# A Fourier filter of eight sequences and a top-k expert layer: transform stages packed differently, gate logits taken from the spectrum, outputs built only for the kept tokens

## The chip, the cores and the metric

One core of one Trainium2 chip runs the whole program: TensorE (PE, with PEld for its weight loads), VectorE (DVE), ScalarE (ACT), GpSimd (POOL), SyncE (SP) and 16 DMA engines. The metric is the device time of one execution in microseconds (us), median of several runs. All data are float32 in DRAM, and products that matter are float32 on TensorE.

## The reference

Eight sequences of 2496 tokens with 256 channels pass through a global filter (a real Fourier transform along the tokens, a product with a filter per frequency and channel, the transform back). The result, 19968 tokens, goes to a layer of 8 experts. Each token's expert is the largest of 8 logits; each expert keeps at most 80 tokens, those of the largest gate value; every other output row is zero.

```python
X = np.fft.rfft(x, axis=1); Y = X * (filt_r + 1j * filt_i)
y = np.fft.irfft(Y, n=2496, axis=1).reshape(19968, 256)
logits = y @ w_gate; expert_idx = argmax(logits); gate_w = softmax(logits)[expert_idx]
for e in range(8):                      # capacity 80
    tok_idx = the 80 tokens of expert e with the largest gate_w
    out[tok_idx] = gate_w[tok_idx] * (relu(y[tok_idx] @ w1[e]) @ w2[e])
```

So at most 640 of the 19968 rows of y are used for more than their logits. In the reference's inputs all eight experts are full (640 kept tokens), and by sequence there are 84, 64, 74, 90, 80, 74, 85 and 89 of them.

## The kernel before

The kernel has three parts: the filter for all sequences (lines 120 to 290), the choice of tokens (`select`, line 369 on), and the experts (lines 309 to 366). Tables for the transforms are made on the host as constants in DRAM and loaded at the start on ACT's DMA queue (`load_tables`, line 150).

A sequence of 2496 = 39 x 64 tokens is transformed in two stages, and back in two. Stage 1 (`stage1`, line 178) takes the transform of length 39: a chunk of x with 78 rows (39 positions by 2 halves h) and 4 columns of 256 channels is the moving side of two matmuls with 512 columns against the constant `wf_t` (78 x 80). The result goes from PSUM (tile `pa`) by DVE or ACT into `t1` and on POOL's DMA queue to a scratch tensor `d1` in DRAM. There are 8 chunks for a sequence. Stage 2 (`load_t2`, line 196, and `stage2`, line 207) reads `d1` back with the 64 positions on the partitions, 128 rows of real and imaginary parts, and works in 10 steps u of two residues s: `pb` is the transform of length 64 (constant `d_t`, 256 moving columns), DVE multiplies it with two copies of the filter (line 222), and `pc` (four matmuls of 256 columns a step, constant `e_t`) is the complex product's sum and the inverse transform of length 64 in one. The result goes to scratch `d2`. Stage 3 (`stage3`, line 246) reads `d2` in 8 chunks of 80 rows: `pd` (512 columns) is the inverse transform of length 39, whose rows go by POOL's queue to `y_rows` in DRAM; `pt` computes the same transposed, with the channels on the partitions, and `pl` takes the 8 logits of each token from that, in 64 matmuls of 8 columns for a sequence. The logits stay in `lg`.

The loop of lines 277 to 290 runs ten rounds: in round i, chunk by chunk, stage 1 of sequence i and stage 3 of sequence i - 2; then stage 2 of sequence i - 1, and then four DMAs that write zeros over that sequence's part of the output (`zero_out`, line 167, POOL's queue, put behind the last write of `d2`). SP's queue loads x, `d1` and `d2`.

After the rounds SP loads weights of five experts, and `select` runs: gates by softmax, keys transposed to (token, expert) rows, a search for the 80th largest key of each expert in 9 steps of 7 counts on DVE (line 482), prefix sums, and a compaction by one-hot products (lines 575 to 593) that leaves for every expert slot the token's number and gate. Then, expert by expert, POOL gathers the 80 rows of `y_rows` by their numbers, two layers run on TensorE, and POOL scatters the rows to the output.

A float32 matmul stands in the trace as two MATMUL instructions, called passes below, each with its LDWEIGHTS.

Of the kernel before, what the change touches and what calls it, by code (L numbers as in the profile page):

```python
# [10 lines left out]
AL = mybir.AluOpType  # L11
# [17 lines left out]
JC = 4  # L29
NCH = NJ // JC  # L30
SG = 4
E, FF = 8, 1024
NDB, NFC = C // 128, FF // 128


def dft_tables():
# [6 lines left out]
    wf = np.zeros((N1, 2, 2, NS, 2))  # L43
    wi = np.zeros((2, NS, 2, N1, 2))
    for h in range(2):
        wf[:, h, :, :, h] = w
        wi[:, :, h, :, h] = v.transpose(0, 2, 1) / S

    # The upper half of q holds the conjugates of frequencies above S / 2.
# [9 lines left out]
    d = d.reshape(128, NS, 128)  # L59
    back = d.transpose(2, 1, 0)  # L60
    e = np.zeros((128, 2, NS, 128))
    e[:, 0] = back
    e[0:64, 1] = back[64:128]
    e[64:128, 1] = -back[0:64]
    f32 = np.float32
    return (wf.reshape(NR, NK).astype(f32), wi.reshape(NK, NR).astype(f32),
            d.astype(f32), e.astype(f32))
# [3 lines left out]
def kernel(  # L71
# [14 lines left out]
    wf_host, wi_host, d_host, e_host = dft_tables()  # L86
# [4 lines left out]
    y_dram = nc.dram_tensor("y_rows", (N, C), F32, kind="Internal").ap()  # L91

    def behind(ins, other):
        tc.add_manual_dep(ins.ins, other.ins.name, mybir.DependencyInfo(
            mybir.DependencyClass.NoSync, mybir.DependencyReason.DATA), reason="order of work")

    consts = ctx.enter_context(tc.tile_pool(name="consts", bufs=1))

# [17 lines left out]
    # Logits of token 2496 b + 32 r + j at [r, 32 b + j, :].  # L116
    T = B * NJ
    lg = consts.tile([NR, T, E], F32, name="lg")

    with ExitStack() as fctx:  # L120
# [5 lines left out]
        xpool = pool("xp", 6)  # L126
        t1pool = pool("t1", 3)
        t2pool = pool("t2", 6)
        xfpool = pool("xf", 2)
        ppool = pool("pp", 4)  # L130
        gpool = pool("gp", 2)
        t4pool = pool("t4", 4)
        ypool = pool("yp", 3)
        ytpool = pool("yt", 2)
        dpool = pool("dram", 2, DRAM)
        fps = pool("fps", 5, PSUM)
        tps = pool("tps", 2, PSUM)
        lps = pool("lps", 1, PSUM)

        wf_t = tpool.tile([NR, NK], F32, name="wf_t")  # L140
        nc.scalar.dma_start(out=wf_t, in_=wf_dram.ap())
        d_t = tpool.tile([128, NS, 128], F32, name="d_t")
        e_t = tpool.tile([128, 2, NS, 128], F32, name="e_t")
        wi_t = tpool.tile([NK, NR], F32, name="wi_t")
        wg = tpool.tile([128, NDB, E], F32, name="wg")
        f_t = [tpool.tile([128, NS, C], F32, name=f"filt{i}") for i in range(2)]
        ZR = S // 4
        zero_t = tpool.tile([128, ZR * C // 128], F32, name="zero_t")

        def load_tables():  # L150
            nc.scalar.dma_start(out=d_t, in_=d_dram.ap())
            for k, filt in enumerate((filt_r, filt_i)):
                for half in range(2):
                    for q in range(2):
                        off, step = (0, C) if q == 0 else (N1 * C, -C)
                        p0 = 64 * half + 32 * q
                        nc.scalar.dma_start(
                            out=f_t[k][p0:p0 + 32],
                            in_=bass.AP(tensor=filt.tensor, offset=filt.offset + off,
                                        ap=[[N1 * C, 32], [step, NS], [1, C]]))  # L160
            nc.scalar.dma_start(out=e_t, in_=e_dram.ap())
            nc.scalar.dma_start(out=wi_t, in_=wi_dram.ap())
            nc.scalar.dma_start(
                out=wg, in_=moe_w_gate.rearrange("(k p) e -> p k e", p=128))
            nc.gpsimd.memset(zero_t[:], 0.0)

        def zero_out(b):
            for i in range(4):
                r0 = b * S + i * ZR
                ins = nc.gpsimd.dma_start(  # L170
                    out=out[r0:r0 + ZR, :].rearrange("r d -> (r d)").rearrange(
                        "(p m) -> p m", p=128),
                    in_=zero_t[:])
                behind(ins, st["last"])

        st = {}

        def stage1(b, ch):
            if ch == 0:
                st["d1", b] = dpool.tile([2 * NS, N2, C], F32, name=f"d1_{b}", tag="d1")  # L180
            d1_rows = st["d1", b].rearrange("a (h n) c -> (a h) n c", h=2)
            xt = xpool.tile([NR, JC, C], F32, name=f"x_{b}_{ch}", tag="x")
            nc.sync.dma_start(
                out=xt,
                in_=bass.AP(tensor=x.tensor, offset=x.offset + (b * S + ch * JC) * C,
                            ap=[[NJ * C, NR], [C, JC], [1, C]]))
# [20 lines left out]
        def stage2(b, u):  # L207
            if u == 0:
                st["d2", b] = dpool.tile([2 * NS, N2, C], F32, name=f"d2_{b}", tag="d2")
# [429 lines left out]
```

## Time and profile before

| | |
|---|---|
| median of 3 runs (lowest, highest) | 1460.03 us (1459.12, 1461.13) |
| span of the profiled execution | 1459.7 us |
| time outside that span, by the median | 0.3 us |
| PE busy / PEld / DVE / ACT / POOL | 1107.9 / 758.3 / 440.0 / 197.6 / 199.0 us |
| bytes moved by DMA | 173.27 MB |
| mean granted clock of TensorE | 0.627 of full speed |

The profile comes from one execution. Busy time is the sum over an engine's instructions; the granted clock is 0.5 for 1.2 GHz and 1.0 for 2.4 GHz, and shows 1.00 before the first change of it is recorded, whatever the clock is. A window's line gives the stretch, its length, the busy us (and instructions) of PE, PEld, DVE, ACT and POOL in it, the granted clock, the DMA share and the GB/s, so a stage can be read by itself. The DMA share is the mean over 16 DMA engines.

### The profile page before, as it was taken

How to read it: one execution, taken by the hardware profiler on the slowest of the kernel's cores; microseconds unless marked ns; L12 is line 12 of the kernel's file. 1: busy time of each engine (PE TensorE's matmuls, PEld its weight loads, DVE VectorE, ACT ScalarE, POOL GpSimd, SP SyncE). 2: the span in 40 equal slices, each digit the busy share in tenths (PEclk: the TensorE clock that was granted, in tenths of full speed). 3: DMA queues.
4: the chain of work that ended last, by engine and by line, in shares of the span. 5: the costliest groups of instructions: out<-in, count | busy, mean ns of one | idle time of the engine just before them, and what ended most of it. 6: DMA issues, size and time to landing. Idle time of an engine off the chain costs nothing. (4 is left out here: it accounts for less than half of the span.)

```text
span 1459.7 us, 10929 instructions
## 1 busy us (share of the span) xinstructions
PE 1107.9 (76%) x4234; PEld 758.3 (52%) x4234; DVE 440.0 (30%) x644; ACT 197.6 (14%) x342; POOL 199.0 (14%) x288
## 2 busy tenths in 40 slices
PE   6395999599969996997899699969969800002497
PEld 1153667466836674666566466747757600001386
DVE  1131113111311140113111311221121189999700
ACT  0121112111301130113011211221121100000001
POOL 1011001100110020002000200010020040001711
PEclk9997557655755585559555855675575555555579
DMA  9986324632563255336433732362162170000050
GB/s 230 236 255 210 107 89 122 199 107 80 142 189 107 80 146 182 98 92 179 150 98 91 222 98 63 88 198 72 35 178 72 59 264 0 0 0 0 7 173 30
DMA packets 71902, 173.27 MB, mean 119 GB/s; under 512 B 8235, under 2 KB 39723, under 8 KB 71467
## 3 DMA queue, kind: packets, MB, share of 16 engines
q0 software_dynamic: 24064, 84.17, 19.5%
q1 hardware_dynamic: 44224, 79.18, 18.5%
q10 hardware_dynamic: 3563, 9.23, 2.8%
q8 instruction: 33, 0.54, 0.2%
q14 instruction: 18, 0.15, 0.0%
HBM read 89.06 MB, written 83.49 MB: 118 GB/s over the span
## 5 line engine op out<-in xcount | busy, mean ns | idle before, releaser
L257 PEld LDWEIGHTS pt<-wi_t,t 80*128 80x128 f32 x1024 | 231.2, 333 | 171.2 <-DMA t<-d 124.5
L257 PE MATMUL pt<-wi_t,t 80*128 80x78 f32 x1024 | 229.8, 419 | 118.5 <-DMA t<-d 118.5
L190 PE MATMUL pa<-x,wf_t 78*80 78x512 f32 x256 | 222.5, 1029 | 35.4 <-ACT t L193 15.6
L263 PE MATMUL pd<-t,wi_t 80*78 80x512 f32 x256 | 231.7, 1061 | 0.0
L268 PEld LDWEIGHTS pl<-wg,yt 128*78 128x78 f32 x1024 | 152.2, 257 | 76.5 <-issue 76.5
L193 DVE COPY t<-pa 80x512 f32<-80x512 f32 x96 | 65.6, 686 | 393.2 <-PE pa L190 349.2
L259 DVE COPY yt<-pt 128x312 f32<-128x312 f32 x128 | 61.8, 482 | 387.2 <-PE pt L257 387.2
L265 ACT COPY y<-pd 78x512 f32<-78x512 f32 x128 | 74.4, 581 | 620.0 <-PE pd L263 620.0
L233 PE MATMUL pc<-p,e_t 128*128 128x256 f32 x640 | 156.0, 386 | 0.6 <-DVE p L222 0.5
L268 PE MATMUL pl<-wg,yt 128*78 128x8 f32 x1024 | 141.9, 274 | 0.0
L222 DVE TENSOR_TENSOR p<-xf,filt 128x512 f32<-128x512 f32 x160 | 103.4, 688 | 109.5 <-ACT xf L218 109.5
L233 PEld LDWEIGHTS pc<-p,e_t 128*128 128x128 f32 x640 | 121.8, 193 | 23.3 <-DVE p L222 6.6
L190 PEld LDWEIGHTS pa<-x,wf_t 78*80 78x80 f32 x256 | 57.0, 246 | 129.1 <-issue 81.4
L270 POOL DMA_DIRECT2D y_rows<-y x64 | 34.0, 531 | 533.1 <-ACT y L265 533.1
L214 PE MATMUL pb<-t,d_t 128*128 128x256 f32 x320 | 97.8, 436 | 0.0
L263 PEld LDWEIGHTS pd<-t,wi_t 80*78 80x78 f32 x256 | 57.4, 255 | 76.4 <-issue 76.4
L482 DVE TENSOR_SCALAR_CACHE_REDUCE junk<-keyT,thr 128x1248 bf16<-128x1248 f32 x63 | 95.3, 1512 | 5.2 <-ACT keyT L451 3.0
L487 PE MATMUL pc<-cnt,grp 128*128 128x7 f32 x18 | 5.3, 365 | 105.1 <-DVE junk L482 105.1
L242 POOL DMA_DIRECT2D d<-g x80 | 50.0, 629 | 197.8 <-ACT g L238 189.4
L214 PEld LDWEIGHTS pb<-t,d_t 128*128 128x128 f32 x320 | 70.4, 223 | 12.5 <-issue 1.1
L194 POOL DMA_DIRECT2D d<-t x64 | 33.4, 523 | 294.6 <-ACT t L193 159.7
L238 ACT COPY g<-pc 128x512 f32<-128x512 f32 x80 | 46.8, 585 | 99.0 <-PE pc L233 97.2
(112 smaller groups left out, 469.2 us busy)
## 6 DMA issues: line engine op xcount, KB each, us to landing
d<-t POOLq DMA_DIRECT2D x64, 320.0 KB, 3.7
t<-d SPq DMA_DIRECT2D x80, 256.0 KB
d<-g POOLq DMA_DIRECT2D x80, 256.0 KB, 3.8
t<-d SPq DMA_DIRECT2D x64, 320.0 KB
x<-in_x_dram SPq DMA_DIRECT2D x64, 312.0 KB
out_dram<-zero_t POOLq DMA_DIRECT2D x32, 624.0 KB, 8.0
y_rows<-y POOLq DMA_DIRECT2D x64, 312.0 KB, 3.3
w<-in_moe_w_dram SPq DMA_DIRECT2D x16, 1024.0 KB
```

Source lines behind the costliest of these rows:

```text
L190: nc.tensor.matmul(out=ps[0:NK], lhsT=wf_t, rhs=xt[:, 2 * i:2 * i + 2, :], start=True, stop=True)
L193: copy(out=t1[:, 2 * i:2 * i + 2, :], in_=ps[0:NK])
L214: nc.tensor.matmul(out=ps[:, i, :], lhsT=d_t[:, s, :], rhs=st["t2", b, s // SG][:, s % SG, :], start=True, stop=True)
L222: nc.vector.tensor_tensor(out=pt, in0=xf, in1=f_t[k][:, 2 * u:2 * u + 2, :], op=AL.mult)
L233: nc.tensor.matmul(out=ps[:, i, :], lhsT=e_t[:, k, s, :], rhs=pr[k][:, i, :], start=(k == 0), stop=(k == 1))
L242: st["last"] = nc.gpsimd.dma_start(out=st["d2", b][a0:a0 + SG].rearrange("s n c -> n s c"), in_=st["g"][64 * p:64 * p + 64])
L257: nc.tensor.matmul(out=pt[:, j, :], lhsT=t4[:, j, 128 * cb:128 * cb + 128], rhs=wi_t, start=True, stop=True)
L259: nc.vector.tensor_copy(out=yt[:, cb], in_=pt)
L263: nc.tensor.matmul(out=ps[0:NR], lhsT=wi_t, rhs=t4[:, 2 * i:2 * i + 2, :], start=True, stop=True)
L265: nc.scalar.copy(out=yr[:, 2 * i:2 * i + 2, :], in_=ps[0:NR])
L268: nc.tensor.matmul(out=pl[0:NR, JC * ch + j, :], lhsT=yt[:, cb, j, :], rhs=wg[:, cb, :], start=(cb == 0), stop=(cb == NDB - 1))
L482: nc.vector.tensor_scalar(out=junk[:], in0=keys, scalar1=thr[:, j:j + 1], scalar2=None, op0=AL.is_ge, op1=AL.add, accum_out=cnt[:, j:j + 1],)
```

## The change

Stage 1 takes 117 rows (39 positions by 3 parts h of 22 columns) against a constant with 120 columns, in six chunks (five of 4 columns, one of 2), so 11 matmuls of 512 columns for a sequence instead of 16. A chunk of x is loaded by three DMAs of 39 rows. Its results are all copied by ACT and written on ACT's DMA queue.

Stage 2 swaps the sides: a 128-channel block of `t2` is the weight side and `d_t` (128 columns) the moving side, so the spectrum comes out with the channels on the partitions. The filter, turned once into this form by 80 transposes, is multiplied on DVE straight from PSUM, and POOL does the two sums of the complex product. A new step `turn`, two steps u later, multiplies with `gi`, which is the identity (128 columns) beside the 8 gate columns: one matmul of 136 columns turns the spectrum back and also takes its product with `w_gate`. ACT copies both, POOL adds the two halves of the gate product into `z` and writes the spectrum to `yf` in DRAM. Stage 3, `y_rows` and the scratch `d2` are gone. Instead `logits`, for two sequences at a time and 16 columns, takes the inverse transform of the gate product alone, in five parts laid between the steps of a later sequence.

The order of all this is written out by hand: in step u of sequence b, stage 2 of b, stage 1 of sequence b + 1 (u below 6), `turn` of step u - 2, from u = 7 the loads of `t2` of b + 1, and a part of `logits`.

The zeros are written after this loop, 32 DMAs on SP's queue; three experts' weights are loaded behind them and the next two after the new stage below. `select` works on 128 partitions (two blocks of 39 used) and has more at its end: which of 128 places of its sequence a kept token takes, and lists of the tokens by sequence.

New between `select` and the experts: `back`, once for each sequence. It gathers the 128 rows (2560 floats each) of a table of the inverse transform that belong to the sequence's kept tokens, loads the sequence's spectrum `yf` (2.6 MB), transposes the gathered rows (20 transposes, copied by DVE and ACT in turn), and 20 matmuls of 256 columns give y for those 128 places, written to `y_sel`. Where a sequence has over 128 kept tokens, a branch taken at run time (`tc.If`) does up to four more lists, each with all eight sequences. The experts gather from `y_sel`.

```diff
-NR = 2 * N1
-NK = 4 * NS
+H3, J3 = 3, 22
+NP1, NM1 = N1 * H3, 2 * NS * H3
+CHUNKS = [(0, 4), (4, 4), (8, 4), (12, 4), (16, 4), (20, 2)]
...
         def stage1(b, ch):
...
+            for i in range(jn // 2):
                 ps = fps.tile([128, 2, C], F32, name=f"pa_{b}_{ch}_{i}", tag="f")
+                nc.tensor.matmul(out=ps[0:NM1], lhsT=wf_t, rhs=xt[:, 2 * i:2 * i + 2, :],
                                  start=True, stop=True)
-                copy = nc.scalar.copy if i == 1 and ch % 2 else nc.vector.tensor_copy
-                copy(out=t1[:, 2 * i:2 * i + 2, :], in_=ps[0:NK])
-            nc.gpsimd.dma_start(out=d1_rows[:, JC * ch:JC * ch + JC, :], in_=t1)
+                nc.scalar.copy(out=t1[:, 2 * i:2 * i + 2, :], in_=ps[0:NM1])
+            nc.scalar.dma_start(out=st["d1", b][:, j0:j0 + jn, :], in_=t1[:, 0:jn, :])
...
         def stage2(b, u):
...
+            for i in range(2):
+                s = 2 * u + i
+                for cb in range(NDB):
+                    nc.tensor.matmul(
+                        out=ps[:, i, cb], rhs=d_t[:, s, :], start=True, stop=True,
+                        lhsT=st["t2", b, s // SG][:, s % SG, 128 * cb:128 * cb + 128])
+            for k in range(2):
...
+                nc.vector.tensor_tensor(
+                    out=pt, in0=ps[:].rearrange("p s c r q -> p (s c) r q"),
+                    in1=f.unsqueeze(2).to_broadcast([128, 2 * NDB, 2, NQ]), op=AL.mult)
...
+            nc.gpsimd.tensor_tensor(out=yt[:, :, 0, :], in0=pr[0][:, :, 0, :],
+                                    in1=pr[1][:, :, 1, :], op=AL.subtract)
+            nc.gpsimd.tensor_tensor(out=yt[:, :, 1, :], in0=pr[0][:, :, 1, :],
+                                    in1=pr[1][:, :, 0, :], op=AL.add)
...
+        def turn(b, u):
...
+                    nc.tensor.matmul(
+                        out=ps[:, i, 136 * cb:136 * cb + 136], rhs=gi[:, cb, :],
+                        lhsT=yt[:, 2 * i + cb].rearrange("p r q -> p (r q)"),
+                        start=True, stop=True)
...
+            nc.scalar.copy(out=ys[:, m:m + 2, :], in_=ps[:, :, 0:ZW])
...
+                nc.gpsimd.dma_start(out=yf[b][:, SG * g:SG * g + SG, :], in_=ys[:, :, E:E + C])
...
+            for b in range(B):
+                for u in range(NU + LATE):
+                    if u < NU:
+                        stage2(b, u)
+                    if b + 1 < B and u < len(CHUNKS):
+                        if xs:
+                            load_x(*xs.pop(0))
+                        stage1(b + 1, u)
+                    if u >= LATE:
+                        turn(b, u - LATE)
+                    if b + 1 < B and u >= len(CHUNKS) + 1 and u - len(CHUNKS) - 1 < NS // SG:
+                        load_t2(b + 1, u - len(CHUNKS) - 1)
+                    if b % 2 == 0 and b > 0 and u in (1, 2, 4, 5, 7):
+                        logits(b // 2 - 1, (1, 2, 4, 5, 7).index(u))
+            for part in range(5):
+                logits(B // 2 - 1, part)
...
+    def back(mp, mps, nm, loads, put, idx, start=True, stop=True, acc=None, pad=False):
...
+        nc.gpsimd.indirect_dma_start(
+            out=gt[:], out_offset=None, in_=rows[:, :],
+            in_offset=bass.IndirectOffsetOnAxis(ap=idx, axis=0), **kw)
+        yb = loads()
...
+        for g in range(NS // SG):
...
+                nc.tensor.transpose(ps[:, i, :], gt[:, 128 * s:128 * s + 128], ident[:])
+            copy = nc.vector.tensor_copy if g % 2 == 0 else nc.scalar.copy
+            copy(out=wt[:, SG * g:SG * g + SG, :], in_=ps[:])
...
+        for s in range(NS):
+            nc.tensor.matmul(po[:], lhsT=wt[:, s, :], rhs=yb[:, s, :],
+                             start=(start and s == 0), stop=(stop and s == NS - 1))
...
+        n_more = nc.values_load(more[0:1, 0:1], min_val=0, max_val=E * cap)
+        with tc.If(n_more > 0):
...
+                for t in range(NX):
+                    ix = spill_lists(tc, mp, mps, t, cap, nof, ohb, iota, idxg)
+                    for b in range(B):
+                        po = back(mp, mps, f"x{t}_{b}",
...
-            out=xg[:], out_offset=None, in_=y_dram[:, :],
+            out=xg[:], out_offset=None, in_=y_sel[:, :],
```

## Rows read from the trace of the kernel before

**Rows 1.** Windows by stage; engines' busy us (instructions), then clock, DMA share, GB/s.
```profile
0.00:91.80 91.80, 56.37 (x65) 15.57 (x66) 16.72 (x28) 5.16 (x8) 10.31 (x25) 1.00 0.94 240
280.00:374.60 94.60, 94.60 (x313) 59.38 (x314) 14.58 (x26) 11.62 (x20) 7.90 (x15) 0.50 0.33 96
374.60:405.70 31.10, 30.98 (x129) 25.17 (x128) 14.13 (x23) 11.60 (x20) 5.94 (x11) 0.91 0.54 147
405.70:420.00 14.30, 0.16 (x1) 0.16 (x1) 0.60 (x1) 0.00 (x0) 2.98 (x6) 0.56 0.99 323
1163.60:1381.20 217.60, 32.49 (x314) 27.16 (x314) 199.24 (x233) 3.58 (x5) 47.17 (x22) 0.50 0.14 50
1381.20:1459.70 78.50, 66.32 (x400) 56.60 (x400) 6.53 (x16) 7.25 (x16) 14.88 (x16) 0.83 0.31 98
```

**Rows 2.** Timeline of PE: start us, us, line, shapes, passes, idle before and its releaser.
```profile
66.11 25.89 PE L190 MATMUL pa<-x,wf_t 78*80 78x512 f32 x30 [3.72 <-DVE t L193]
...
234.43 3.76 PE L214 MATMUL pb<-t,d_t 128*128 128x256 f32 x8
...
244.27 1.89 PE L233 MATMUL pc<-p,e_t 128*128 128x256 f32 x8
246.00 1.03 PE L214 MATMUL pb<-t,d_t 128*128 128x256 f32 x4
...
280.00 3.70 PE L257 MATMUL pt<-wi_t,t 80*128 80x78 f32 x16 [14.70 <-DMA t<-d]
...
1386.41 13.86 PE L332 MATMUL ph<-xs,w 128*128 128x80 f32 x64
...
1413.64 3.69 PE L332 MATMUL ph<-xs,w 128*128 128x80 f32 x32
```

**Rows 3.** Groups by line and shape: busy us, mean ns of one, idle before and releasers.
```profile
L222 DVE TENSOR_TENSOR p<-xf,filt 128x512 f32<-128x512 f32 x160 | 103.4, 688 | 109.5 <-ACT xf L218 109.5
L265 ACT COPY y<-pd 78x512 f32<-78x512 f32 x128 | 74.4, 581 | 620.0 <-PE pd L263 620.0
L242 POOL DMA_DIRECT2D d<-g x80 | 50.0, 629 | 197.8 <-ACT g L238 189.4 <-issue 8.5
L465 POOL TENSOR_TENSOR res<-gw,vv 78x256 f32<-78x256 f32 x1 | 0.8, 809 | 0.1
L449 PE MATMUL pk<-ident,key 78*128 78x78 f32 x16 | 2.3, 339 | 24.8 <-issue 24.8
L424 DVE TENSOR_TENSOR sh<-lg,mx 78x2048 f32<-78x2048 f32 x1 | 2.3, 2286 | 0.0
L599 DVE SCALAR_TENSOR_TENSOR tok<-slot,tok 80x8 f32<-80x8 f32 x1 | 0.2, 164 | 0.0
```

**Rows 4.** Windows of 1 us after which the clock is high, in stage 2 and among the experts.
```profile
240.00:241.00 1.00, 1.00 (x5) 0.85 (x5) 0.14 (x1) 0.00 (x0) 0.00 (x0) 0.93 0.92 278
1404.00:1405.00 1.00, 1.00 (x6) 0.74 (x5) 0.00 (x0) 0.00 (x0) 0.00 (x0) 0.95 0.54 217
```

**Rows 5.** DMA queues of the page: packets, MB, share of 16 engines' span.
```profile
q0 software_dynamic: 24064, 84.17, 19.5%
q1 hardware_dynamic: 44224, 79.18, 18.5%
```

**Rows 6.** Two windows without any compute, DMA alone (columns as in Rows 1).
```profile
268.00:272.00 4.00, 0.00 (x0) 0.00 (x0) 0.00 (x0) 0.00 (x0) 0.40 (x1) 0.50 1.01 386
274.00:278.00 4.00, 0.00 (x0) 0.00 (x0) 0.00 (x0) 0.00 (x0) 0.00 (x0) 0.50 1.03 287
```

**Rows 7.** Timeline of ACT at the start: its queue issues the tables.
```profile
1.77 25.48 ACTq L157 DMA_DIRECT2D filt<-in_filt_r_dram  x4
```

**Rows 8.** The experts' gathers of 80 rows of 1 KB, issue to landing.
```profile
DMA to landing us min/median/max: 2.5/4.0/5.9
```

**Rows 9.** Timeline of POOL: the last scatter, the last instruction before the end.
```profile
1452.73 0.91 POOL L350 DMA_INDIRECT out_dram<-ys,idxs  x1 [2.54 <-ACT ys L349]
```

**Rows 10.** POOL's elementwise product of the compaction, all calls: shortest, median, longest ns.
```profile
L580 POOL TENSOR_TENSOR vals<-vv,oh_bf x8: 2758/5335/5337, 1193.1 to 1369.7; 78x1536 bf16<-78x1536 bf16 x8
```

More of the change, by code (lines that the diff above doesn't have):

```diff
@@ L42, in dft_tables @@
     v[0, :, 0], v[1, :, 0] = 1.0, 0.0
[L43 to L47, printed above, removed]
+    v /= S
+    wf = np.zeros((H3, N1, 2, NS, H3))
+    for h in range(H3):
+        wf[h, :, :, :, h] = w
     kap = np.where(q[:, None] < 32, s + N1 * q[:, None], s + N1 * (95 - q[:, None]))
@@ L150, in load_tables @@
[L150 to L153, printed above, removed]
+        t2pool = pool("t2", 8)
+        ppool = pool("pp", 2)
+        ytpool = pool("yt", 3)
+        yspool = pool("ysp", 3)
+        zpool = pool("zp", 2)
+        d1pool = pool("d1p", 3, DRAM)
+        fps = pool("fps", 4, PSUM)
+        yps = pool("yps", 2, PSUM)
+        wf_t = tpool.tile([NP1, NM1], F32, name="wf_t")
@@ new lines, with load_tables @@
+        d_t = tpool.tile([128, NS, 128], F32, name="d_t")
+        e_t = tpool.tile([128, NS, 128], F32, name="e_t")
+        wi_t = tpool.tile([NS, 2, N1], F32, name="wi_t")
+        gi = tpool.tile([128, 2, 128 + E], F32, name="gi")
+        ft = [tpool.tile([128, NS, NDB, NQ], F32, name=f"ft{i}") for i in range(2)]
+        fst = [stg.tile([NQ, NS, C], F32, name=f"fst{i}") for i in range(2)]
+        def load_tables(part):
+            if part == 0:
+                nc.scalar.dma_start(out=wf_t, in_=wf_dram.ap())
+            elif part == 1:
+                for k, filt in enumerate((filt_r, filt_i)):
@@ L162, in load_tables @@
[L162 to L174, printed above, removed]
@@ L299, in load_weights @@
         nc.sync.dma_start(out=w2s[e], in_=moe_w2[e].rearrange("(k p) d -> p k d", p=128))
-    for e in range(5):
+    for i in range(4 * B):
+        nc.sync.dma_start(
+            out=out[i * ZR:i * ZR + ZR, :].rearrange("r d -> (r d)").rearrange(
+                "(p m) -> p m", p=128),
+            in_=zero_t[:])
+    for e in range(3):
         load_weights(e)
@@ L354, in layer2 @@
         )
+    for e in range(3, 5):
+        load_weights(e)
     gather(0)
@@ new lines, in select @@
+        for b in range(1, B):
+            nc.vector.tensor_tensor(out=over[:, b + 1:b + 2], in0=over[:, b + 1:b + 2],
+                                    in1=over[:, b:b + 1], op=AL.add)
+        nc.vector.tensor_copy(out=more[:], in_=over[0:1, B:B + 1])
+        b128 = sp.tile([cap, B], F32, name="b128")
+        nc.vector.tensor_scalar(out=b128[:], in0=iota[0:cap, 0:B], scalar1=128.0, scalar2=None,
+                                op0=AL.mult)
+        jump = sp.tile([cap, B], F32, name="jump")
```

462 lines of the change are left out of this document (303 added, 159 removed).

## The prediction

> **What bounds the kernel now.** I read the windows by stage first. A full round of the loop lasts 140 us (280 to 420) and has three parts [rows 1]: 94.6 us of stages 1 and 3, PE busy throughout at the low clock (0.50, which is 1.2 GHz); 31.1 us of stage 2, PE busy, clock mostly 1.00 (2.4 GHz); and 14.3 us in which no engine computes while the DMA share is 0.99. The timeline names that last wait: PE stands until `d2` is read back [rows 2]. The chain of waits of this page ends after three steps and says nothing here. After 1163.6 us come 217.6 us of token choice, of which DVE is busy 199, and 78.5 us of experts [rows 1].
>
> So TensorE sets the first 80% of the time, and DVE then the choice. What the change makes shorter is in the first part; it adds to the second and puts a new stage behind it.
>
> The price of a pass follows from the timeline [rows 2]. `pa`, 512 columns, took 25.89/30 = 863 ns at 1.2 GHz. `pc`, 256 columns, started 8 passes in 246.00 - 244.27 = 1.73 us, 216 ns at 2.4 GHz. `ph` has only 80 columns but weights of 128, and took 13.86/64 = 217 ns at 1.2 GHz and 3.69/32 = 115 ns at 2.4 (110 without the last one's drain). So a pass costs two cycles for each moving column or each weight column, whichever are more, and I price the new matmuls so.
>
> **TensorE after the change, for a sequence, two passes to a matmul.** Stage 1: 11 matmuls of 512 columns, 22 x 431 ns = 9.5 us at the high clock. Spectrum: 40 matmuls of 128 on 128 columns, 80 x 110 = 8.8. `turn`: 40 of 136 columns, 80 x 115 = 9.2. `logits` for two sequences: 40 passes x 110 + 16 transposes (72 ns, half of the 2.3/16 = 145 ns that `pk` took at 0.50 [rows 3]) + 8 x 431 = 9.0, so 4.5 for one. Sum 32.0 us at the high clock, twice that, 64, at the low one. Before it was about 126 us of a 140 us round.
>
> **Which clock.** `pa`, 78 rows deep, kept PE busy for 25.89 us without a gap and its passes stayed at 1.2 GHz; `ph` did so for 13.86 us [rows 2]. The clock was at 0.93 in the window from 240, after `pb` and `pc` passes (128 rows, 256 columns) had run since 234.4, and at 0.95 in that from 1404, after `ph` had given way at 1400.3 to the second layer's 256 columns; later `ph` passes among the experts ran at the high clock [rows 2, 4]. The new passes are like `pb` and `pc`: 117 or 128 rows deep, moving side busy all the time. I take the high clock for most of a sequence, and 5.6 us at the low one after the wait at a seam, which costs 2.8, say 3 us. Both ends stay: 32 us and 64 us.
>
> The Trainium skill (TensorE: Matmul & The Clock Gate, "Why this matters for your kernels") says that keeping TensorE continuously busy gets it to the high clock. The trace contradicts that as a sufficient condition: `pa` was busy for 25.89 us at 863 ns a pass. By the page alone the rival of a low clock, below, would have no place.
>
> **The other engines, for a sequence** [rows 3]. DVE: 20 products of 512 elements x 0.69 = 14 us. ACT: 11 + 10 copies x 0.58 = 12 us, and six DMA issues of about 0.4. POOL is new on this path: 40 sums of 256 elements, 20 steps' halves in pairs; in 10 steps two each, 20 x 0.81 = 16.2, five issues x 0.63 and five small sums of about 0.3, together 21 us. All lie under 32 us, but in steps 6 to 9, where no stage 1 runs, PE needs 1.8 us and POOL 2.0, so POOL paces there; with the hand-over PE, DVE, POOL, PE I take 5 us of waits for a sequence (0 to 12).
>
> **DMA, for a sequence.** x 3 x 39 x 22 KB = 2.64 MB, `d1` written 2.70, read 2.62, `yf` written 2.62: 10.6 MB. The two main queues moved 163.4 MB in 38.0% of the span, 294 GB/s while busy [rows 5], so 36 us; windows with nothing but DMA ran at 287 and 386 [rows 6], so 27 to 37 us. That is about PE's time: neither hides fully under the other.
>
> The Trainium skill (DMA: Bandwidth & Descriptors, "Why a DMA increments its semaphore by 16 and not by 1") says a hardware-queue DMA uses the largest number of engines up to 16 that divides its outer dimension. That makes 13 engines for a 39-row load of x (and 13 for the 78 rows of before) and 15 for the 120-row write of `d1`, so an estimate of 38.5 us instead of 36, inside the bounds above; no view here shows it.
>
> The seam: `d1`'s last chunk must land before `t2` is read, and `t2` before the next sequence's step 0. In the old seam the 14.3 us [rows 1] hold 2.56 MB of zeros (8.7 us at 294), so write and read back cost about 5.6; the new one has steps 6 to 11 as cover, 9 us of PE work. I take 4 us for what is late (0 to 8). One sequence then: 32 + 3 + 5 + 4 = 44 us (36 to 68).
>
> **Start and end of the loop.** The first stage 2 now begins at 91.8 us [rows 1]. ACT's queue was held 25.48 us by the first four filter DMAs [rows 7]; those stay, the other four and half of `e_t` go. ACT can copy from about 28 us; 11 chunk halves paced by `pa` (1.73 us for two passes) end near 43, write and read back take 6, the filter's 80 transposes x 145 ns = 11.6 run meanwhile, and four more us for hand-over: 58 us (45 to 75). Sequences 0 to 6: 7 x 44 = 308. Sequence 7 has no stage 1 beside it and goes at POOL's pace: 24. The last `logits`, 9 us at the high clock, 18 at the low, with copies: 17. The loop ends at 58 + 308 + 24 + 17 = 407 instead of 1163.6.
>
> **Token choice.** The 217.6 us stay: DVE's instructions have the same free sizes on more partitions. New at the end are some 40 DVE instructions of 0.16 to 0.2 us [rows 3], one of 1024 elements (1.2, half of the 2.29 for 2048), and matmuls with about 5 us: 15. The zeros (20.4 MB, 70 us at 294) and 6.3 MB of weights go in here, where the DMA share is 0.14 and nothing waits; two spectra follow them. 233 us.
>
> **The new stage.** Per sequence 20 transposes in groups of four, paced by five copies of about 0.7 us: 4 us; then 20 matmuls of 256 columns, 40 x 216 = 8.6. 12.7 us at the high clock, 21.3 at the low; DMA 3.93 MB, 13.4 us at 294, 10.2 at 386. I take 14, as DMA and PE alternate in the lead: 112, and 13 for the first gather and the last write: 125 us (115 to 183). A gather of 1.3 MB isn't in the trace. A gather of 80 KB landed in 4.0 us [rows 8]; at 294 GB/s the new one takes 4.5 us more than such a one's latency, and by bytes alone (80 KB in 4.0 us) 64 us. I take the former, since a row of 80 KB is mostly latency.
>
> **Branch and experts.** No row shows a branch that isn't taken. The nearest is the end of the program, where all engines meet: 6.1 us after the last instruction (1453.6 to 1459.7), a scatter's landing included [rows 9]. 6 us (0 to 15). Experts 78.5; PE comes warm, which spares half of the 13.86 us of `ph` [rows 2], and the weights of experts 3 and 4 now start late (4.2 MB, 14 us, wanted after about 14): 77 (70 to 88).
>
> **Sum:** 407 + 233 + 125 + 6 + 77 = 848 us, against a span of 1459.7; the median of the runs is 0.3 above that span, which I leave out.
>
> **Rivals.** *Low clock all through the loop*: 64 + 4 us a sequence, 7 x 68 + 58 + 38 + 25 = 597 for the loop, and with the rest as above 1038. For it: `pa` and `ph` stayed low when dense [rows 2], and DMA waits break the work up. Against it: `pb` and `pc` rose. *Everything overlaps*: DMA reads at 386, seams vanish, 36 us a sequence, start 50: 50 + 252 + 22 + 12 = 336, then 230 + 115 + 2 + 72 = 755. For it: PE's sum alone is 32. Against it: DMA at 294 alone is 36. *The gathers go by bytes*: 8 x (64 - 14) more, 1248. For it only that no gather of long rows is in the trace. *POOL is slowed*: its product of two inputs took 2758 ns alone and 5335 beside DVE's compare of two inputs from SBUF [rows 10]; twice 21 us is about 42, which moves the sequence to some 50 and the sum to 890, inside the forecast's range. Against it: the new DVE product takes one input from PSUM. *Slower than before*: the branch is taken. Then 32 more rounds, one buffer each, of 13.4 + 4 + 8.6 = 26 us: 832 more, 1680. It decides as soon as one sequence has over 128 kept tokens; the reference's inputs have 64 to 90, so only a wrong count would do it.
>
> **Numbers.** Forecast, 780 to 960: 0.66; low clock in most of the loop, 960 to 1060: 0.16; full overlap below 780: 0.11; gathers by bytes or the like above 1060 but under 1460: 0.05; slower: 0.015. No case lies near no change (within 0.2%, 3 us, is what a measurement of this kernel can't tell from none): 0.005. Range 775 to 1010.
>
> **What would show it.** Right: loop's end near 407; passes of the spectrum at 110 ns in most of a sequence; rounds of about 44 us with PE and DMA both above 0.7; token choice near 233 with the zeros under it; rounds of 14 us in the new stage. Wrong: passes at 217 ns throughout; PE waiting on POOL in every step; gathers landing after tens of us; a stretch between new stage and experts in which no engine works.

## The result and the profile after

The changed kernel takes 774.92 us (770.79 to 776.13, 4 runs) against 1459.57 for the one before (1457.67 to 1461.13, 4 runs): a ratio of 0.53, with a 95% interval from 0.5281 to 0.5318. The prediction was 848, with a range from 775 to 1010; the time lies at the range's low end, 0.08 us below it. The profiled execution has a span of 772.2 us; all stages below are measured on that.

The page, its busy times, slices (19.3 us each), queues and four of its groups (busy us, mean ns | idle before, most of it from):

```profile
span 772.2 us, 8200 instructions
PE 482.4 (62%) x3004; PEld 387.4 (50%) x3004; DVE 362.8 (47%) x519; ACT 123.4 (16%) x210; POOL 226.8 (29%) x302
PE   3258797998899979892100000122431999987996
PEclk9567998999999999985555555555555999995999
DMA  9999999799989997999992000000007789812720
q1 hardware_dynamic: 47222, 101.84, 41.0%
q10 hardware_dynamic: 8624, 26.94, 11.8%
q0 software_dynamic: 7680, 32.77, 11.5%
L241 DVE TENSOR_TENSOR p<-pb,ft 128x512 f32<-128x512 f32 x160 | 102.7, 686 | 156.0 <-issue 91.6
L246 POOL TENSOR_TENSOR yt<-p,p 128x256 f32<-128x256 f32 x80 | 57.9, 724 | 170.5 <-DVE p L241 170.2
L234 PE MATMUL pb<-d_t,t 128*128 128x128 f32 x640 | 88.2, 283 | 22.1 <-DMA t<-d 22.1
L258 PE MATMUL py<-gi,yt 128*128 128x136 f32 x640 | 90.1, 284 | 10.6 <-POOL yt L248 9.9
```

Read the three slice rows together, down the columns. Slices 1 to 18 are the start and the loop: DMA is at 9 nearly throughout; from slice 4 PE is between 7 and 9, from slice 6 the clock at 8 or 9. Slices 19 to 30 are the token choice, where PE has little to do and DMA falls to 0 once the zeros and weights are done. The last ten are the new stage, where after the first gather PE is at 9 and DMA at 7 to 9, and the experts.

The windows by stage (us, then busy us with instructions of PE, PEld, DVE, ACT and POOL, granted clock, DMA share, GB/s): the start, three rounds of the loop (with `logits`, without, with), six rounds together, the last sequence with its tail, then the sequence, a stretch of it and the tail by themselves, the choice, the wait for the first gather, the whole new stage, its middle rounds, the branch, the experts:

```profile
0.00:59.86 59.86, 22.62 (x102) 12.56 (x103) 8.88 (x14) 7.53 (x12) 3.44 (x12) 0.71 0.95 231
131.58:172.68 41.10, 39.55 (x246) 30.84 (x247) 17.53 (x26) 12.38 (x21) 17.79 (x28) 0.92 0.87 261
172.68:207.62 34.94, 30.26 (x184) 23.53 (x183) 12.88 (x20) 13.09 (x22) 19.66 (x32) 0.95 0.94 296
207.62:245.68 38.06, 36.52 (x246) 28.93 (x247) 17.53 (x26) 12.38 (x21) 17.87 (x29) 1.00 0.91 289
95.70:317.69 221.99, 201.77 (x1284) 157.79 (x1285) 91.23 (x138) 75.99 (x128) 112.75 (x179) 0.97 0.93 286
317.69:353.00 35.31, 31.88 (x226) 26.46 (x224) 15.51 (x24) 7.07 (x12) 19.61 (x32) 0.85 1.04 390
317.69:339.10 21.41, 19.28 (x162) 18.56 (x161) 12.80 (x20) 5.51 (x9) 18.64 (x30) 1.00 1.05 375
322.80:336.00 13.20, 13.18 (x114) 12.85 (x112) 8.82 (x15) 4.29 (x7) 12.23 (x21) 1.00 1.02 412
339.10:353.00 13.90, 12.59 (x66) 7.90 (x64) 2.71 (x4) 1.55 (x3) 0.98 (x2) 0.63 1.02 413
353.00:582.50 229.50, 37.66 (x332) 31.69 (x332) 207.60 (x275) 3.59 (x5) 49.64 (x25) 0.50 0.25 93
582.50:598.60 16.10, 0.00 (x0) 0.01 (x1) 0.11 (x1) 0.00 (x0) 2.04 (x2) 0.50 0.94 378
582.50:692.80 110.30, 91.00 (x480) 78.04 (x480) 20.06 (x33) 9.39 (x16) 7.67 (x8) 0.91 0.76 295
611.50:681.00 69.50, 67.14 (x364) 57.65 (x362) 15.09 (x25) 7.04 (x12) 4.70 (x5) 1.00 0.85 333
692.80:697.00 4.20, 0.00 (x0) 0.00 (x0) 0.04 (x1) 0.00 (x0) 0.03 (x1) 1.00 0.13 41
697.00:772.20 75.20, 66.02 (x400) 56.45 (x400) 6.53 (x16) 7.27 (x16) 14.66 (x16) 0.84 0.31 102
```

A round of the loop was 140 us with PE busy for 125.7 of them [rows 1]; now six rounds take 221.99, 37.0 each, with PE busy for 33.6 at a clock of 0.97. PE is the busiest engine in both kernels, but now DMA stands beside it at 0.93. The loop ends at 353.0 instead of 1163.6, a gain of 810.6; the choice takes 11.9 us more, the new stage costs 110.3 and the branch 4.2, and the experts take 3.3 less. The sum is the 687.5 us between the two spans.

In PE's timeline (start, us, shapes, passes, idle before and its releaser) the price of a pass and the few waits that are left are seen:

```profile
131.58 2.05 PE L234 MATMUL pb<-d_t,t 128*128 128x128 f32 x8 [4.81 <-DMA t<-d]
...
246.57 1.88 PE L212 MATMUL pa<-x,wf_t 117*120 117x512 f32 x4
248.29 1.06 PE L234 MATMUL pb<-d_t,t 128*128 128x128 f32 x8
249.18 1.88 PE L212 MATMUL pa<-x,wf_t 117*120 117x512 f32 x4
...
264.03 1.09 PE L212 MATMUL pa<-x,wf_t 117*120 117x512 f32 x2 [1.17 <-DMA x<-in_x_dram]
...
279.64 1.13 PE L234 MATMUL pb<-d_t,t 128*128 128x128 f32 x8 [2.95 <-DMA t<-d]
...
598.62 3.71 PE L398 MATMUL pw<-ident,gt 128*128 128x128 f32 x16 [16.21 <-DMA gt<-rows_tbl,idxb]
...
701.07 13.94 PE L464 MATMUL ph<-xs,w 128*128 128x80 f32 x64
```

Four passes of `pa` start within 248.29 - 246.57 = 1.72 us, 430 ns each instead of 863 [rows 2]. The seam, the first `pb` of a sequence, waits 2.95 us for `t2` at 279.64 and 4.81 at 131.58, the longest such wait inside the loop, where the old kernel waited 14.3. The new stage begins with a wait of 16.21 us for the first gather, with no engine computing. The last row is the experts' first layer, still at 13.94/64 = 218 ns a pass.

### The profile page after: what moved, and what is told of

It reads as the page before. It is cut to its first block, busy times and chain, and to the rows that moved or that the text cites. A ratio compares the mean times of both kernels' runs of the same rounds, so it can differ in the third digit from the quotient of the medians.

```text
span 772.2 us, 8200 instructions
## 1 busy us (share of the span) xinstructions
PE 482.4 (62%) x3004; PEld 387.4 (50%) x3004; DVE 362.8 (47%) x519; ACT 123.4 (16%) x210; POOL 226.8 (29%) x302
## 5 line engine op out<-in xcount | busy, mean ns | idle before, releaser
L241 DVE TENSOR_TENSOR p<-pb,ft 128x512 f32<-128x512 f32 x160 | 102.7, 686 | 156.0 <-issue 91.6
L212 PE MATMUL pa<-x,wf_t 117*120 117x512 f32 x176 | 94.5, 663 | 30.4 <-ACT t L214 17.5
L246 POOL TENSOR_TENSOR yt<-p,p 128x256 f32<-128x256 f32 x80 | 57.9, 724 | 170.5 <-DVE p L241 170.2
L234 PE MATMUL pb<-d_t,t 128*128 128x128 f32 x640 | 88.2, 283 | 22.1 <-DMA t<-d 22.1
L234 PEld LDWEIGHTS pb<-d_t,t 128*128 128x128 f32 x640 | 81.8, 198 | 32.6 <-issue 32.5
L258 PEld LDWEIGHTS py<-gi,yt 128*128 128x128 f32 x640 | 82.9, 192 | 28.3 <-issue 14.2
L258 PE MATMUL py<-gi,yt 128*128 128x136 f32 x640 | 90.1, 284 | 10.6 <-POOL yt L248 9.9
L403 PE MATMUL pr<-yb,wt 128*128 128x256 f32 x320 | 71.7, 379 | 0.0
L214 ACT COPY t<-pa 120x512 f32<-120x512 f32 x88 | 51.3, 586 | 114.2 <-PE pa L212 104.7
L403 PEld LDWEIGHTS pr<-yb,wt 128*128 128x128 f32 x320 | 59.6, 190 | 7.4
L248 POOL TENSOR_TENSOR yt<-p,p 128x256 f32<-128x256 f32 x80 | 57.8, 722 | 0.0
L780 PEld LDWEIGHTS <-ohp 128*80 128x80 bf16 x256 | 17.7, 181 | 40.6 <-DVE ohp L775 40.6
```

The costliest lines, as they stand in the source:

```text
L212: nc.tensor.matmul(out=ps[0:NM1], lhsT=wf_t, rhs=xt[:, 2 * i:2 * i + 2, :], start=True, stop=True)
L214: nc.scalar.copy(out=t1[:, 2 * i:2 * i + 2, :], in_=ps[0:NM1])
L234: nc.tensor.matmul(out=ps[:, i, cb], rhs=d_t[:, s, :], start=True, stop=True, lhsT=st["t2", b, s // SG][:, s % SG, 128 * cb:128 * cb + 128])
L241: nc.vector.tensor_tensor(out=pt, in0=ps[:].rearrange("p s c r q -> p (s c) r q"), in1=f.unsqueeze(2).to_broadcast([128, 2 * NDB, 2, NQ]), ...
L246: nc.gpsimd.tensor_tensor(out=yt[:, :, 0, :], in0=pr[0][:, :, 0, :], in1=pr[1][:, :, 1, :], op=AL.subtract)
L248: nc.gpsimd.tensor_tensor(out=yt[:, :, 1, :], in0=pr[0][:, :, 1, :], in1=pr[1][:, :, 0, :], op=AL.add)
```

## The experiments

The main theory (DMA and PE overlap fully): a round lasts as long as the longer of its DMA and its TensorE work, and neither waits for the other beyond that. The rivals: the hand-over PE, DVE, POOL, PE sets the rounds; the seam of write and read-back does; and, for the gain as a whole, that it is the clock and not the smaller work. A round is counted from the first `pb` pass of a sequence to that of the next; means are of the last six of seven. In the changed kernel these six take 35.88, 41.10, 34.94, 38.06, 33.96 and 38.05 us; the second, fourth and sixth have `logits`.

**The zeros back in the loop**, on GpSimd's queue. DMA gets 2.56 MB more a sequence, PE nothing.

```diff
 (in the loop over b, behind the steps of a sequence)
+                for i in range(4 * b, 4 * b + 4):
+                    nc.gpsimd.dma_start(out=out[i * ZR:i * ZR + ZR, :]..., in_=zero_t[:])
```

> The changed kernel with the zeros written inside the loop again, four DMAs of 640 KB behind each sequence's steps on GpSimd's queue (2.56 MB more in a round of 10.6 MB). Theory 1 (a round lasts as long as the longer of its DMA and its TensorE passes; DMA leads in rounds without logits, TensorE in those with): rounds of 35 us become 42 to 44, rounds of 38 become 42 to 44, the loop ends 45 to 60 us later and the total is 815 to 835 us. Theory 2 (a chain of hand-overs TensorE, VectorE, GpSimd, TensorE and the read back at the seam set the round; DMA has room): rounds lengthen by GpSimd's 2.2 us of issues at most, total 775 to 795 us.

815.36 us (811.28 to 816.95), a ratio of 0.5582 [0.5561, 0.5602]. The window of six rounds:

```profile
95.92:353.61 257.69, 210.83 (x1285) 163.29 (x1286) 91.15 (x138) 75.70 (x128) 122.91 (x200) 0.90 0.94 303
```

The round grows from 37.0 to 42.95 with the same instructions on PE. DMA carries 303 GB/s here at a share of 0.94, while PE is busy for 0.82 of the time, and each of the six rounds has grown, by 4.5 to 9.0 us: DMA sets the mean round, though single rounds take 39.66 to 45.86. 13.2 MB at 303 is 43.6 us. By the same rate the 10.6 MB of the changed kernel need 35.0. That the zeros were moved is worth 40 us, for the choice hides them.

**One sequence's x for all**, so that sequences 1 to 7 load none, 2.64 MB a round less.

```diff
 def load_x(b, ch):
+            if b > 0:
+                return
 ...
-            xt = st.pop(("x", b, ch))
+            xt = st["x", 0, ch]
```

> The changed kernel with x of sequence 0 loaded once and used for all eight sequences: this leaves out the loads of the other seven, 2.64 of 10.6 MB in a round, with all else as before (the values of the seven other sequences are those of the first). Theory 1: rounds without logits fall from 35 us to TensorE's 30 to 32, rounds with logits stay at TensorE's 37 to 38; total 750 to 765 us. Theory 2: rounds stay at 35 and 38; total 770 to 778 us.

741.04 us (740.29 to 743.13), 0.5084 [0.5071, 0.5097], a little less than expected, since the loop also starts 8 us earlier (first `pb` at 51.64 instead of 59.86).

```profile
51.64:284.42 232.78, 224.31 (x1467) 177.52 (x1467) 104.06 (x158) 88.56 (x149) 131.64 (x209) 0.99 0.86 242
```

DMA, 7.95 MB or 26.2 us, is now the shorter side, and the rounds become regular: 29.15, 37.98, 29.16, 37.98, 29.15, 37.98. That is TensorE's own round, without `logits` and with, 33.57 in the mean, and PE is busy for 224.31 of 232.78 us.

**Five of the eleven stage 1 matmuls left out**: PE loses 5 x 2 x 430 ns = 4.3 us a round, DMA nothing.

```diff
+                if i == 1:
+                    ps = st["pa"]
+                else:
                     nc.tensor.matmul(out=ps[0:NM1], lhsT=wf_t, rhs=xt[:, 0:2, :], ...)
```

> The changed kernel with the second of the two stage-1 matmuls of a chunk left out, its copy made from the first one's result: 5 of 11 matmuls of 512 columns less, 4.3 us of TensorE in a round, all DMAs and copies the same. Theory 1: rounds without logits stay at 34 to 36 us, those with logits fall from 38 to DMA's 35 to 36; total 763 to 773 us. A rival by which TensorE alone sets every round: 4 us less in each, total 740 to 748 us. Theory 2: total 765 to 778 us.

768.56 us (766.04 to 769.76), 0.5271 [0.5259, 0.5282].

```profile
94.70:310.28 215.58, 178.06 (x1226) 148.36 (x1225) 91.27 (x138) 73.66 (x129) 113.71 (x181) 0.94 0.96 296
```

PE is busy for 24 us less in six rounds, and they are 6.4 us shorter. PE alone doesn't set them either.

**Both cuts together.**

> Both reductions together: x of sequence 0 for all, and 5 of 11 stage-1 matmuls left out. Theory 1: both limits fall, to 27 us of DMA and 28 us (33 with logits) of TensorE; rounds of 29 to 33 us; total 725 to 750 us, more than the sum of the two single effects where each alone was held by the other limit. Theory 2: rounds stay at 33 us or more; total 765 to 778 us.

715.62 us (714.37 to 716.8), 0.4902 [0.4891, 0.4913], below the 725 to 750 expected; this loop too starts 8 us earlier, at 51.75, and its mean round, 30.0, is in the 29 to 33 expected.

```profile
79.25:259.52 180.27, 169.20 (x1226) 143.10 (x1225) 91.17 (x138) 73.14 (x129) 113.55 (x181) 1.00 0.92 273
```

The cuts bring 34 us and 6 us alone and 59 together; taken over the seven rounds alone, without the earlier start, 25, 9 and 50. Two sides that limit by turns do this; a chain of waits that adds up would not. The rounds are 27.43, 33.76, 25.39, 33.76, 26.16, 33.77: near DMA's 26.2 without `logits`, PE's 37.98 - 4.3 = 33.7 with them.

**One of POOL's two sums given to DVE**, so that POOL has half as many sums in the hand-over.

```diff
-            nc.gpsimd.tensor_tensor(out=yt[:, :, 1, :], ...
+            nc.vector.tensor_tensor(out=yt[:, :, 1, :], ...
```

> The changed kernel with one of GpSimd's two sums of the complex product moved to VectorE: GpSimd's 18 to 20 us in a round become 11 to 13, VectorE's 13 become about 20. Theory 1 (DMA and TensorE set the rounds): total 768 to 780 us. Theory 2 (the hand-overs over GpSimd set the rounds): rounds 2 to 4 us shorter, total 745 to 762 us.

772.35 us (768.96 to 774.35), 0.5295 [0.5285, 0.5305]; the round is 36.9.

```profile
L246 POOL TENSOR_TENSOR yt<-p,p 128x256 f32<-128x256 f32 x80 | 69.4, 867 | 197.3 <-DVE p L241 196.3 <-PE pb L234 0.8
L248 DVE TENSOR_TENSOR yt<-p,p 128x256 f32<-128x256 f32 x80 | 34.0, 425 | 2.8
```

The sum left on POOL takes 867 ns beside DVE's, instead of 724, so POOL's sums fall from 115.7 to 69.4 us, not by half. The interval overlaps that of the changed kernel: no difference is shown, where 2 to 4 us a round were expected if the hand-over set the rounds. That rival falls. POOL's 170 us of idle time before `yt` in the page are the wait of an engine with time to spare.

**`logits` spread** over even and odd sequences, two parts and three, with the same work.

```diff
-                    if b % 2 == 0 and b > 0 and u in (1, 2, 4, 5, 7):
-                        logits(b // 2 - 1, (1, 2, 4, 5, 7).index(u))
+                    if b % 2 == 0 and b > 0 and u in (1, 5):
+                        logits(b // 2 - 1, (1, 5).index(u))
+                    if b % 2 == 1 and b > 1 and u in (1, 4, 7):
+                        logits(b // 2 - 1, 2 + (1, 4, 7).index(u))
```

> The changed kernel with the five parts of the logits of a pair spread over two rounds (two parts in the even one, three in the odd one) instead of all in the even one; nothing else differs. If a round lasts as long as the longer of DMA (about 34.6 us) and TensorE (29.2 us without logits, 38.0 with): rounds of 34 and 38 us become all 35 to 36, the loop is 6 to 12 us shorter, total 762 to 770 us. Rival (only the sum of TensorE's and DMA's work counts, whatever round it lies in): total 772 to 778 us.

766.15 us (759.92 to 768.93), 0.5256 [0.5239, 0.5273]. The window of six rounds:

```profile
92.34:302.62 210.28, 195.37 (x1260) 154.25 (x1261) 86.60 (x132) 76.10 (x128) 112.92 (x179) 0.98 0.96 299
```

No round is above 35.44 in this execution; the mean is 35.05, DMA's time. TensorE's peak of 38 in every second round was what DMA's time in the others could not make good. The execution that was traced is the fastest of the four, at 759.92 us; by the medians the spread brings 8.8 us, and 35.05 is the round at its best.

The six runs beside the rule, in us. DMA is the MB of a round over 303 GB/s, where the first row with zeros gives that rate itself; PE is 29.15 and 37.98, less 4.3 where matmuls are left out:

```
kernel              DMA    PE without / with logits   mean of the longer   measured
changed             35.0   29.2 / 38.0                36.5                 37.0
zeros in the loop   43.6   29.2 / 38.0                43.6                 42.95
x shared            26.2   29.2 / 38.0                33.6 (from it)       33.6
stage 1 cut         35.0   24.9 / 33.7                35.0                 35.9
both cuts           26.2   24.9 / 33.7                30.0                 30.0
logits spread       35.0   33.6 in the mean           35.0                 35.05
```

The rule holds for the mean to within about 1 us; single rounds scatter around it, with the stage 1 cut from 32.04 to 40.15. In the changed kernel the 0.5 us between 36.5 and 37.0 are one round, 131.58 to 172.68: the seam ahead of it waited 4.81 us, the clock then began low (eight `pb` passes in 2.05 us instead of 1.06, 0.92 in the whole round), and with the work of the rounds of 38.06 and 38.05 it took 41.10. So in one round of six a wait and the low clock did come on top.

**The kernel before with 128 rows deep contractions.** Stages 1 and 3 contract over 78 and 80 rows; here rows of zeros fill both operands to 128. The passes, their columns and the result stay.

```diff
-        wf_t = tpool.tile([NR, NK], F32, name="wf_t")
+        wf_t = tpool.tile([128, NK], F32, name="wf_t")
+        nc.vector.memset(wf_t[:], 0.0)
+        xbuf = [tpool.tile([128, JC, C], F32, name=f"xbuf{i}") for i in range(6)]
+        t4buf = [tpool.tile([128, JC, C], F32, name=f"t4buf{i}") for i in range(4)]
+        for t in xbuf + t4buf:
+            nc.vector.memset(t[64:128], 0.0)
 (wi_t likewise; x and t4 are loaded into these buffers)
```

> The kernel before, with the stage 1 and stage 3 matmuls that contract over 78 or 80 rows made 128 rows deep: rows of zeros below x, d2 and their two tables, in buffers cleared once. Passes, columns, DMAs and results are the same. Theory (the clock is held low by shallow contractions): the 94.6 us block of stages 1 and 3 in a round, at 0.50 before, reaches the high clock for most of its time, so 50 to 65 us; rounds of 140 become 95 to 115; total 1060 to 1270 us. Rival (the clock depends on how many columns move, or on TensorE being busy, and rows of zeros change nothing): total 1450 to 1465 us.

1129.49 us (1126.66 to 1132.53), 0.7734 [0.7713, 0.7755]. The block of stages 1 and 3 and the rest of that round in the windows, then PE's timeline:

```profile
330.49:382.97 52.48, 52.48 (x317) 34.69 (x317) 14.60 (x26) 11.62 (x20) 7.37 (x15) 0.93 0.56 166
382.97:426.43 43.46, 28.29 (x127) 23.06 (x126) 14.65 (x23) 11.61 (x20) 9.43 (x16) 0.89 0.80 222
```

```profile
243.49 1.92 PE L194 MATMUL pa<-xbuf,wf_t 128*80 128x512 f32 x4
245.25 1.91 PE L261 MATMUL pt<-wi_t,t4buf 128*128 128x78 f32 x16
...
251.55 1.91 PE L261 MATMUL pt<-wi_t,t4buf 128*128 128x78 f32 x16
```

The block takes 52.5 us instead of 94.6 [rows 1], the clock in it is 0.93 instead of 0.50, and a pass of `pa` takes 1.76/4 = 440 ns. The seam is still there in the second window: 43.46 us of which PE is busy 28.3.

**The same buffers, 78 and 80 rows again**, for control.

> A control for the kernel before with 128-row contractions: the same fixed buffers for x and d2 and the same clearing of them, but the matmuls of stages 1 and 3 contract over their 78 and 80 rows again. If the depth brings the clock: the block of stages 1 and 3 is back at 94 to 95 us and 0.50, total 1450 to 1470 us. Rival (the fixed buffers and their order of loads made it faster): total 1130 to 1250 us.

1468.22 us (1467.52 to 1468.67), 1.0052 [1.0033, 1.0072].

```profile
286.90:381.93 95.03, 95.03 (x316) 59.80 (x317) 14.58 (x26) 11.62 (x20) 7.88 (x15) 0.50 0.33 98
```

The depth of the contraction did it, not the fixed buffers. So 330 of the 685 us can be had from the clock alone, with all of the old work. 128 rows did not bring it everywhere: `ph`, 128 rows deep, ran 13.86 us at the low level in the kernel before [rows 2] and 13.94 in the changed one. The Trainium skill (TensorE: Matmul & The Clock Gate, "Why this matters for your kernels") has continuous work as the way to the high clock; this block was continuously busy for 95 us at 0.50, and with zeros added it ran at 0.93, so here the measurement decides: being busy was not enough.

**The kernel before with the zeros behind the loop**, to see what they cost in the old seam.

```diff
-                zero_out(i - 1)
 (and behind the loop, on SyncE's queue)
+    for i in range(4 * B):
+        nc.sync.dma_start(out=out[i * ZR:i * ZR + ZR, :]..., in_=zero_t[:])
```

> The kernel before with one part of the change alone: the zeros written behind the loop on SyncE's queue, ahead of the experts' weights, as in the changed kernel. If the 14.3 us of waiting in a round were 8.7 us of zeros ahead of the read of d2: the wait falls to 5 to 6 us in the rounds that have it, total 1385 to 1405 us. Rival (the read of d2 waits for its own writes and TensorE's cold start, the zeros only lie beside it): total 1440 to 1460 us.

1420.89 us (1419.84 to 1425.92), 0.973 [0.9714, 0.9746], between both expectations. One seam of eight:

```profile
273.87 3.70 PE L254 MATMUL pt<-wi_t,t 80*128 80x78 f32 x16 [8.57 <-DMA t<-d]
```

Seven of the eight seams wait 8.4 to 9.8 us, where the kernel before has 13.5 to 17.8; the eighth, at 948.47, still waits 14.86, for a reason not looked into. The zeros cost about 5.5 us in a seam, the write and read-back about 9. The prediction had 8.7 and 5.6.

**The first two spectra loaded during the choice**, into buffers of their own; three buffers of weights instead of five make room.

```diff
+    ybs = [spectrum(ybp, b, f"{b}") for b in range(2)]
     select(tc, lg, cap, ident, ...
 ...
-        lambda: spectrum(mp, b, f"{b}")
+        lambda: ybs[b] if b < 2 else spectrum(ybp, b, f"{b}")
```

> The changed kernel with the spectra of the first two sequences loaded during the token choice, into buffers of their own set up ahead of it (the pool of expert weights has three buffers instead of five for that). If the 16 us from the list of tokens to the first transposes are the first gather beside 5.2 MB of spectra that start only then: the first gather lands after 6 to 8 us instead of 14, and the total is 762 to 770 us, unless the weights of experts 3 and 4, which now wait for a free buffer, give some back. Rival (the gather by itself takes those 14 us): total 770 to 785 us.

763.0 us (762.29 to 768.13), 0.5235 [0.5214, 0.5256].

```profile
586.45 3.90 PE L408 MATMUL pw<-ident,gt 128*128 128x128 f32 x16 [7.90 <-DMA gt<-rows_tbl,idxb]
```

The wait for the first gather is 7.90 us instead of 16.21. In the changed kernel the spectra's buffers reuse memory of the choice, so their loads are issued at 582.54, together with the gather, and compete with it. The intervals don't touch: this version beats both kernels. Of the 12 us between the two traces 8.3 are this wait; the other 3.9 lie before the choice's end, and executions of the changed kernel differ by as much among themselves (770.79 to 776.13).

**This and the spread `logits` together.**

> The logits spread over two rounds and the first two spectra loaded during the token choice, both at once. The two lie in different stages, so their gains add: 763 us less the 6 to 12 of the spread logits, 750 to 758 us. Rival (no gain from the spread): 762 to 767 us.

763.38 us (756.78 to 769.4), 0.5216 [0.5191, 0.524]. The expected 750 to 758 was missed, and the time lies where the rival put it. The interval overlaps that of each of the two alone, so it isn't shown that the gains add; why the spread shows no gain on top here stays open.

**One spectrum for all lists**: seven loads of 2.6 MB are left out of the new stage.

```diff
     def spectrum(mp, b, nm):
+        if b > 0 and nm == f"{b}":
+            return st0[0]
```

> The changed kernel with the spectrum of sequence 0 loaded once in the new stage and used for all eight lists: this leaves out seven loads of 2.6 MB. If TensorE sets the 11.6 us rounds of that stage (transposes and 256-column passes at the high clock): rounds stay at 11.6 us, and only the first gather may land earlier, total 765 to 776 us. Rival (spectrum loads pace the stage): rounds of 8 to 10 us, total 745 to 760 us.

766.58 us (765.63 to 767.52), 0.5253 [0.5241, 0.5264]. Three of the eight rounds in DVE's timeline:

```profile
604.72 0.42 DVE L407 COPY yr<-pr 128x256 f32<-128x256 f32 x1 [7.51 <-PE pr L403]
...
616.24 0.42 DVE L407 COPY yr<-pr 128x256 f32<-128x256 f32 x1 [7.51 <-PE pr L403]
...
627.81 0.42 DVE L407 COPY yr<-pr 128x256 f32<-128x256 f32 x1 [7.51 <-PE pr L403]
```

627.81 - 616.24 = 11.57, the round of the changed kernel too. The spectra's loads don't set it; TensorE does (busy for 67.14 of 69.50 us in the middle rounds of the changed kernel). The whole gain lies ahead of the first round, whose copy of `yr` begins at 604.72 instead of 611.44; 3.7 us of that are the first gather, waited for 12.53 us here, the rest lies before the choice's end, where this edit changes nothing.

## Why the prediction was right, and where it was wrong

The direction, the high clock and most prices held; in the loop's round waits were added up that for the most part overlap. The terms of the sum, against the profiled span:

```
                                predicted   measured   difference
start, to the first spectrum    58          59.9       +1.9
seven rounds                    308         257.8      -50.2
last sequence and logits tail   41          35.3       -5.7
token choice                    233         229.5      -3.5
new stage                       125         110.3      -14.7
branch                          6           4.2        -1.8
experts                         77          75.2       -1.8
sum                             848         772.2      -75.8
```

**The step that failed** is "One sequence then: 32 + 3 + 5 + 4 = 44 us". TensorE's 32 was close: 33.6 with x shared. The other 12 us were three waits added to it as if they came one after another. Measured without DMA's limit, the low clock and the hand-over together are 33.6 - 32 = 1.6 us, not 8: the clock is 0.97, and PE waits 9.9 us for `yt` in all eight sequences, 1.2 in one, as other passes are ready while a `yt` is made. The seam's 4 us are no term for every round either. PE's waits for `t2` are 22.1 us in the page: 9.35 before the first sequence, and 1.62 to 4.81 in four of the seven rounds. What comes on top of TensorE's 33.6 is 3.4, since DMA's 35.0 is longer in rounds without `logits` and TensorE's 38.0 in those with; that gives 36.5, and the round of 41.10, the one in which the seam and the low clock came as I had said, the last 0.5. I had both sums, 32 and 36, and wrote "neither hides fully under the other"; the runs show that in five rounds of six each does.

The rival "everything overlaps" had the round, 36 us, and was right in its mechanism, though not by the rate that it gave for it: the loop's rounds didn't move 386 GB/s, but 303 where DMA alone set them. Its shorter start (50) and experts (72) were wrong, the forecast's (58, 77) right; its last sequence with tail (34) and new stage (115) were nearer than the forecast's. So the time came out between the two, 20 us above the rival's 755. Its chance, 0.11, was too small: the only row against it, DMA at 294 alone for 36 us, was itself a round of 36.

**The clock** was right. It is at 0.97 in the loop; `pa` passes take 430 ns and those of `pb` 0.89/8 = 111 (110 predicted). I had put it down to passes that are "117 or 128 rows deep, moving side busy all the time"; the padded version of the kernel before shows the depth by itself, at the same moving columns, and its control that the buffers don't bring it. The low clock as a rival falls with it. Among the experts the clock was wrong: "PE comes warm, which spares half of the 13.86 us of `ph`" did not happen, as `ph` took 13.94 us again. That the experts still came out near 77 (75.2) is luck; where the gain there comes from was not looked into.

**DMA.** 36 us for a sequence stood against 35.0. The estimate of 38.5 by the Trainium skill (DMA: Bandwidth & Descriptors, "Why a DMA increments its semaphore by 16 and not by 1") comes to 38.7 when worked out again, and isn't borne out as a time: with spread `logits`, at a DMA share of 0.96, a round takes 35.05. How many engines a load used, no view here shows.

**POOL** was priced at 0.81 us a sum and takes 0.72; that it would set the pace in steps 6 to 9 isn't seen in the time, as taking half of its sums away changed nothing. In the changed kernel it wasn't slowed by DVE, so that rival falls too; it was where DVE got the other sum (867 ns), from SBUF on both inputs. In the last sequence, where it was said to set 24 us, the sequence took 21.4 and the tail 13.9 instead of 17. From 322.80 to 336.00 PE was busy for 13.18 of 13.20 us and POOL for 12.23, so there too PE led, if closely.

**The new stage.** Its round was 14, "as DMA and PE alternate in the lead"; it is 11.57, and PE leads alone. DMA moved 333 GB/s there at a share of 0.85, so it had room left, and with seven of the loads gone the round was the same. The gather landed in 10.2 us in the median for 1.3 MB: more than the 8.5 that I took, far below the 64 by bytes. The choice has a mistake that did cost time: "two spectra follow" the zeros and weights there, but their buffers aren't free until the choice ends. The first gather then cost a wait of 16.2 us, 8.3 more than with the early loads, and what the 13 for "the first gather and the last write" stood for took 110.3 - 8 x 11.57 = 17.7; the stage came out under 125 because its rounds were short.

**Zeros.** That the choice would hide them was right: 229.5 us with 0.25 of the DMA time used. Their price in the old seam was too high (5.5, not 8.7), which by itself moved no term, since the new seam was taken by judgement.

Where the 685 us come from, in the order clock, then work: the padded kernel's round is 95.9 us (52.5 + 43.5) against 140, which is the clock, 330 us over the kernel; from there to 37.0 is smaller and overlapped work, 810.6 - 330 = 480 in the loop, of which the choice, the new stage and the branch take back 126. Another order would divide it otherwise. What packing and the product on the spectrum bring each was not tried apart.

## What to carry to other kernels

Where two resources need about the same time for a stage and the work is buffered deeply enough, take the longer of the two for each round, not a sum with waits; then look whether the longer one changes from round to round, for evening it out costs no work (8.8 us here by the medians, though nothing more was shown on top of the early spectra). Before a gain is put down to less arithmetic, look at the granted clock: here half of it was to be had by rows of zeros. A load that is to be early must have a buffer that is free early; look at its issue in the timeline, not at the order of the code.

## What was not expected of the hardware

- Rows of zeros in the contraction raised the granted clock of this block: the same passes, 78 and 80 rows deep, ran for 95.03 us at 0.50, and padded to 128 rows for 52.5 at 0.93. How deep it must be was not tried, and 128 rows did not do it for the 13.94 us of `ph`.
- The rate of DMA differs from stage to stage: 303 GB/s in the rounds that it sets, 333 in the new stage, 378 in the 16 us before that and 390 in the last sequence with the first zeros, at shares of 0.94, 0.85, 0.94 and 1.04. What in the transfers makes the difference was not tried.
